# A speech joint's forward and backward pass on one core: row-layout fe by a transposing transfer, stores of out on GpSimd's queue, own tile for the g gradient, x ahead of grad_out, last w1 gradients together

## The chip, the cores and the metric

The kernel runs on one core of a Trainium2 chip. Times are device microseconds (us) of one execution. The core has TensorE (PE in the profile, with its weight loads as PEld), VectorE (DVE), ScalarE (ACT), GpSimd (POOL) and SyncE (SP), and sixteen DMA engines. A DMA is issued by SP, ACT or POOL; the transposing DMAs of this kernel are all issued by SP.

## The reference

Two strided convolutions over time with gelu, a joint of the result f with a second sequence g, and all gradients for a given grad_out:

```python
h = sum_i einsum(xp[:, i:i+T], w1[i]);  h = gelu(h)[:, ::2]
f = sum_i einsum(hp[:, i:i+T1], w2[i]); f = gelu(f)[:, ::2]
fe = f @ w_f          # (B, 4000, 256)
ge = g @ w_g          # (B, 8, 256)
j = tanh(fe[:, :, None] + ge[:, None])
out = j @ w_o         # (B, 4000, 8, 256)
# returned: out and the gradients of x, w1, w2, g, w_f, w_g, w_o
```

B = 2, T = 16000, D = 256, three taps, U = 8 rows of g, all bf16.

## The kernel before

**Tiling.** The 2 x 4000 rows of f are taken as one line of 8000 and cut into 17 chunks: one of 256, fifteen of 512, one of 64. Chunk 8 holds the border of the two batches. A chunk's rows stand in blocks of 128 (4 blocks in a full chunk). The channel axis has two halves of 128.

**Stages of a chunk.** `stage_a` (lines 500 to 564) does both convolutions, gelu and its derivative factors (G1o, G1e, G2), then fe with channels on partitions (tile FE), and from chunk 2 on (`NTR = 2`) calls `fe_rows`, which turns FE into rows (tile FER) by 8 TensorE transposes at line 575 and one eviction. HT, the activations, is turned into rows HR by a transposing DMA (`tile_rows`, line 485). `stage_j` (line 614) runs four times over pairs of u: tanh of FE with ge as bias (JT, line 630); the same tanh in row layout (JR): for chunks 0 and 1 by TensorE transposes of JT, later by adding FER and the broadcast ge rows GEB (line 653) and a tanh (line 658); the products for w_o's gradient (GWO), for the gradient of j (from GOT, grad_out transposed by a DMA), and for out, which is evicted into OUT_SB and stored (line 730) by SP. Buffers JR are 3, OUT_SB 3, GOT 3, grad_out (GO) 4. `stage_de` (line 796) does the backward convolutions: GN, its rows GNR by a transposing DMA, GH and its rows GHR, the weight gradients of w_f and w2 (`wgrad`), the gradient of x (GX_SB, stored by SP), and calls `grad_w1` (line 933) from x in rows (XR) and GHR. Each weight gradient is a PSUM sum of one chunk that VectorE adds into an fp32 accumulator (line 777); the last one is subtracted from the negated accumulator into a STAGE tile (line 768) and stored.

In the loop over k from line 1065 the body runs `stage_j` of chunk k, `stage_a` of chunk k + 1 and `stage_de` of chunk k - 1. After the last chunk, `grad_w1` of chunk 15 is run as the final one; that of chunk 16 comes before it as an ordinary accumulation.

**Order of the work.** Nothing is issued where it is written. Every operation is recorded with its engine, a cost, its data dependences and a due time, and `Flow.issue` (line 106) simulates the engines and the SP queue and emits the instructions in the order that the simulation gives. For SP it knows three kinds of transfers, T (transposing), L (load) and S (store), with bytes per ns, gaps between kinds (`TURN`) and a backlog limit per kind. That order is fixed at build time; at run time each engine takes its instructions in that order and waits for semaphores. A buffer of a class (`cls`, line 50) is used again once its last user is done.

**Other names.** GpSimd copies the halos, the block edges that a convolution reads from a neighbour (`halo`, line 414; the copies are at line 347). `make_ge_rows` (587) and `gg_out` (954) make the rows of ge and the gradient of g; both take a buffer of class `jr` for their small result. `load_xc` (360) loads x transposed (XC), chunk 1 in two parts; `load_go` and `load_got` load grad_out and transpose it; `load_xr` loads x as rows. At the start W1 and W2 come as six loads on ACT's queue. `evac` (317) moves PSUM to SBUF on ACT or DVE; all matmuls are recorded at line 312 (`mm`).

Of the kernel before, what the change touches and what calls it, by code (L numbers as in the profile page):

```python
# [20 lines left out]
class Buf:  # L21


    def __init__(self, cls, shape, dtype, name):
        self.cls, self.shape, self.dtype, self.name = cls, shape, dtype, name
        self.t, self.slot, self.log, self.users, self.seq, self.born = None, None, [], 0, None, None
# [5 lines left out]
class Op:  # L32
    __slots__ = ("eng", "cost", "fn", "deps", "succ", "left", "prio", "new", "bufs", "done", "xfer", "n", "ready")


class Flow:
# [4 lines left out]
    TURN = {"TL": 800.0, "TS": 800.0, "SL": 550.0, "LL": 350.0}  # L41
# [20 lines left out]
    def op(self, eng, cost, fn, r=(), w=(), new=(), at=None, xfer=None, after=()):  # L62
# [23 lines left out]
        deps.update(b.born for b in bufs if b.born is not None)  # L86
# [13 lines left out]
    def ring(self, prev, kind, work):  # L100

        if kind == "T":
            return (1.3 * work + 250.0, 0.0) if prev == "T" else (work, 0.0)
        return work, self.TURN.get((prev or "") + kind, 130.0)

    def issue(self):
# [6 lines left out]
        def put(o):  # L113
            o.ready = max((d.done for d in o.deps), default=0.0)
            for e in o.eng:
                avail[e].append(o)
# [4 lines left out]
        while left:  # L121
# [54 lines left out]
            for b in o.bufs:  # L176
                b.users -= 1
                if b.users == 0 and b.cls is not None:
                    slots[b.cls][b.slot][1] = o.done
# [29 lines left out]
def kernel(  # L209
# [28 lines left out]
    KT = 2  # L238
# [30 lines left out]
    for name, n in (("xc", 1), ("ht", 1), ("g1e", 2), ("g1o", 2), ("g2", 2), ("fe", 2),  # L269
                    ("fer", 2), ("gsq", 2), ("gs", 2), ("jt", 3), ("got", 3), ("go", 4), ("out", 3), ("jr", 3),  # L270
# [36 lines left out]
    NGR = fixed([U, B, D], BF16, "NGR")  # L307
    gT = [fixed([P, KT, U], BF16, f"gT{b}") for b in range(B)]
# [23 lines left out]
    def dma(q, out, in_, r, w, bytes_, new=(), transpose=False, load=False, at=None, after=(), land=1500.0):  # L332
# [6 lines left out]
        if transpose:  # L339
            c, work = 1020.0 + bytes_ / 1100.0, bytes_ / 306.0  # L340
        else:
            c, work = 600.0, bytes_ / 384.0
        c = {"SP": c, "POOL": 650.0, "ACT": 450.0}[q]
        return op(q, c, go, r=r, w=w, new=new, at=at, after=after, xfer=("T" if transpose else "L" if load else "S", work, land))
# [15 lines left out]
    def load_xc(g_, at, after=()):  # L360
# [4 lines left out]
        for n_, (b0, b1) in enumerate(cuts):  # L365
            dma("SP", lambda b0=b0, b1=b1: XC[:, b0:b1, :, :c.np].rearrange("p j k n -> p (j k) n"),
                lambda b0=b0, b1=b1: dram(xf, 4 * c.q0 - 1 + b0, 4 * c.nb, b1 - b0, c.np),
                r=[], w=[(XC, ("m", n_))], bytes_=(b1 - b0) * c.np * D * 2, new=[XC] if n_ == 0 else [], transpose=True, at=at,
                after=after, land=2500.0 if c.first else 1500.0)
# [6 lines left out]
    def load_go(g_, up, at, after=()):  # L376
# [4 lines left out]
            bytes_=c.W * 1024, new=[GO], load=True, at=at, after=after)  # L381
        st[g_].setdefault("GO", {})[up] = GO

    def load_got(g_, up, at):
# [3 lines left out]
        dma("SP", lambda: GOT[:, 0:c.nb, :, :, :c.np].rearrange("p a j k n -> p (a j k) n"),  # L388
# [4 lines left out]
    def load_xr(g_, at, after=()):  # L393
# [5 lines left out]
        if c.first:  # L399
            pool_zero(lambda: XR[0:1, 0:3, :], [], [(XR, "a")], new=[XR], at=at, n=768)  # L400
            dma("SP", lambda: XR[0:1, 3:nr, :].rearrange("p f d -> p (f d)"), lambda: dram(xf, 0, 24, nr - 3, 1),
                r=[], w=[(XR, "b")], bytes_=3072, load=True, at=at, after=after)
            for lo, hi in ((1, 16), (16, 128)):
                dma("SP", lambda lo=lo, hi=hi: flat(lo, hi), lambda lo=lo, hi=hi: dram(xf, r0 + 8 * lo, 8, nr, hi - lo),
                    r=[], w=[(XR, lo)], bytes_=(hi - lo) * nr * 512, load=True, at=at, after=after)
        else:
            dma("SP", lambda: flat(0, c.np), lambda: dram(xf, r0, 4 * c.nb, nr, c.np),
                r=[], w=[(XR, "m")], bytes_=c.np * nr * 512, new=[XR], load=True, at=at, after=after)
# [20 lines left out]
    def conv_gelu(g_, jobs, rd, h_buf, pre, ho, gname, gcls, gshape, gsave, news):  # L429
# [4 lines left out]
        if c.first:  # L434
# [18 lines left out]
        for mt in range(KT):  # L453
# [11 lines left out]
        G = buf(gcls, gshape, BF16, gname)  # L465
# [13 lines left out]
            out=full(G, go_), in0=full(s, so), in1=full(sq), op=ALU.mult), r=both(sk) + both(qk), w=[(G, ("g", 0)), (G, ("g", 1))], new=[G], at=late)  # L479
# [20 lines left out]
    def stage_a(g_, t0, dt):  # L500
# [50 lines left out]
        FE = S["FE"] = buf("fe", [P, KT, CW], BF16, "FE")  # L551
        for mt in range(KT):
# [6 lines left out]
            evac(lambda mt=mt: FE[:, mt, :c.W], lambda ps=ps: ps[:, :c.W], c.W, r=[ps], w=[(FE, mt)])  # L559
# [6 lines left out]
    def fe_rows(g_):  # L566
        c, S = chunks[g_], st[g_]
        nb, n_, FE = c.nb, c.np, S["FE"]
        FER = S["FER"] = buf("fer", [P, NB, D], BF16, "FER")
        ps = psum(BF16)  # L570

        def trs(e, ps=ps):
            for a in range(nb):
                for kt in range(KT):
                    nc.tensor.transpose(out=ps[:n_, (a * KT + kt) * P:(a * KT + kt + 1) * P],  # L575
                                        in_=FE[:, kt, a * n_:(a + 1) * n_], identity=ident[:])
# [10 lines left out]
    def make_ge_rows():  # L587

        rows = buf("jr", [P, 2, 2, D], BF16, "JR")
        for b in range(B):  # L590
# [5 lines left out]
            op("PE", c_pe([D] * 2), mms, r=[gT[b], WG], w=[ps], new=[ps] + ([rows] if b == 0 else []))  # L596
            evac(lambda b=b: rows[:U, b, 0], lambda ps=ps: ps[:U, :D], D, r=[ps], w=[(rows, b)])
        dma("POOL", lambda: GED[:].rearrange("b (u d) -> u b d", d=D), lambda: rows[:U, :, 0, :], r=[rows], w=[GED],
            bytes_=8192, land=2500.0)

    def load_geb(c, at):
        t_ = lambda: GED[:]
        for up in range(UP):
            for lo, hi, b in parts_of(c):
# [3 lines left out]
                    r=[GED], w=[(GEB, up)], bytes_=(hi - lo) * 1024, load=True, at=at(up))  # L608
# [5 lines left out]
    def stage_j(g_, t0, dt):  # L614
# [4 lines left out]
        def cut(ap, lo, hi):  # L619
            return ap.rearrange("p (a n) -> p a n", a=nb)[:, :, lo:hi] if c.mid else ap  # L620

        def pair(up):
# [4 lines left out]
            for j in range(2):  # L627
                for mt in range(KT):
                    for k_, (lo, hi, b) in enumerate(parts_of(c)):
                        op("ACT", c_act((hi - lo) * nb, ptr=True), lambda e, j=j, mt=mt, lo=lo, hi=hi, b=b: nc.scalar.activation(  # L630
                            out=cut(JT[:, j, mt, :W], lo, hi), in_=cut(S["FE"][:, mt, :W], lo, hi), func=ACT.Tanh,
# [98 lines left out]
            dma("SP", lambda dst_=dst_: dst_, lambda OUT=OUT: OUT[:n_, 0:nb].rearrange("p a u v -> p a (u v)"), r=[OUT], w=[],  # L730
# [65 lines left out]
    def stage_de(g_, t0, dt):  # L796
# [84 lines left out]
        load_xr(g_, t0 - 300.0 if c.last else t0 + dt * 0.3)  # L881
# [51 lines left out]
    def grad_w1(g_):  # L933
        c, S = chunks[g_], st[g_]
        nb, nx = c.nb, c.nx
        XR, GHR = S["XR"], S["GHR"]
        rows = lambda R, a, d2, m: R[:m, a, d2 * P:(d2 + 1) * P]
# [186 lines left out]
```

## Time and profile before

| | |
|---|---|
| median of three runs | 791.5 us (787.8 to 792.93) |
| the profiled execution | 793.2 us |
| its span, first to last instruction | 791.3 us, granted TensorE clock 0.992 |
| DMA in the span | 184.34 MB, mean 233 GB/s |
| SP's queue (q1) | 182.16 MB, 99.2% of 16 engines' time |
| GpSimd's queue (q0) | 0.41 MB |

Costly groups of instructions, by shape, with busy time and mean:

| line, engine | what | count | busy us | mean ns |
|---|---|---|---|---|
| L630 ACT | tanh JT from FE, 128x512 | 224 | 156.5 | 746 |
| L312 PE | out from JT and WO, 256 columns | 992 | 149.3 | 273 |
| L698 DVE | NGZ from JSQ and PSUM, 128x512 | 196 | 132.5 | 677 |
| L713 DVE | ZS + NGZ, fp32 128x1024 | 90 | 109.4 | 1215 |
| L653 DVE | JR from FER and GEB | 112 | 76.0 | 683 |
| L575 PE | transposes of FE | 112 | 8.5 | 219 |
| L321 ACT | FER from PSUM, 128x1024 | 14 | 14.5 | 1037 |

A matmul's duration overlaps with the next one's, so the spacing of starts says more of TensorE's pace than the mean. A wait for several semaphores is put down to the one that came last. In views by window the numbers after each engine's busy time are counts.

### The profile page before, as it was taken

What the parts mean: (1) busy time and instruction counts of PE and PEld (TensorE: products, weight loads), DVE (VectorE), ACT (ScalarE), POOL (GpSimd) and SP (SyncE); (2) the same over time, 40 slices, a digit from 0 to 9 for tenths busy, and PEclk for the clock granted to TensorE, in tenths of its full rate; (3) what the DMA queues carried; (4) which work ended last, traced back from release to release, by engine and by line L of the source; (5) the groups of instructions that cost most, each with busy time, mean ns of one, the idle gap of its engine ahead of it and who ended that gap; (6) DMA issues with size and microseconds to landing.
All of it is one profiled execution on the core that took longest, in us unless ns stands there. A gap on an engine that the chain in (4) does not pass through costs nothing. (4 is left out here: it accounts for less than half of the span.)

```text
span 791.3 us, 15382 instructions
## 1 busy us (share of the span) xinstructions
PE 770.7 (97%) x5620; PEld 534.6 (68%) x5620; DVE 725.1 (92%) x1519; ACT 711.1 (90%) x1134; POOL 88.2 (11%) x225
## 2 busy tenths in 40 slices
PE   8989989999999999999999998999999999999996
PEld 5756657676676766767566674676767667677765
DVE  4889989999999999999998987999999999999875
ACT  5999989989999999999999897998999999999752
POOL 3101110110102011010100201002020010201000
PEclk9999999999999999999999999999999999999999
DMA  9999999999999999999999999999999999899563
GB/s 204 236 239 223 232 226 257 236 234 277 226 283 222 245 247 221 259 222 255 253 229 251 244 268 230 208 257 214 272 243 239 247 219 276 196 247 249 156 180 94
DMA packets 396084, 184.34 MB, mean 233 GB/s; under 512 B 320350, under 2 KB 389768, under 8 KB 394088
## 3 DMA queue, kind: packets, MB, share of 16 engines
q1 hardware_dynamic: 394136, 182.16, 99.2%
q10 hardware_dynamic: 1632, 0.79, 0.4%
q8 instruction: 44, 0.72, 0.4%
q0 software_dynamic: 240, 0.41, 0.2%
q14 instruction: 32, 0.26, 0.1%
HBM read 52.99 MB, written 50.35 MB: 131 GB/s over the span
## 5 line engine op out<-in xcount | busy, mean ns | idle before, releaser
L630 ACT ACTIVATE JT<-FE,GE 128x512 bf16<-128x512 bf16 (+4 forms) x288 | 183.0, 686 | 0.1
L312 PE MATMUL ps<-WO,JT 128*128 128x256 bf16 (+1 forms) x1008 | 151.8, 273 | 0.3 <-DVE JR L326 0.2
L698 DVE SCALAR_TENSOR_TENSOR NGZ<-JSQ,ps 128x512 f32<-128x512 bf16 (+3 forms) x252 | 151.2, 607 | 0.4 <-PE ps L312 0.2
L312 PE MATMUL ps<-GOT,WOT 128*128 128x512 bf16 (+2 forms) x544 | 150.6, 362 | 0.8 <-ACT FE L321 0.4
L312 PEld LDWEIGHTS <-JT 128*128 128x128 bf16 (+1 forms) x1008 | 98.5, 98 | 62.1 <-issue 0.8
L321 ACT CAST OUT_SB<-ps 128x512 bf16<-128x512 f32 x200 | 119.8, 600 | 17.6 <-PE ps L312 17.1
L689 ACT ACTIVATE JSQ<-JT 128x1024 bf16<-128x1024 bf16 (+2 forms) x127 | 128.8, 1014 | 6.4 <-DVE NGZ L698 6.0
L312 PE MATMUL GWO<-GO_R,JR 128*128 128x256 bf16 (+1 forms) x1008 | 132.2, 274 | 0.0
L658 ACT ACTIVATE JR<-JR 128x1024 bf16<-128x1024 bf16 (+1 forms) x116 | 123.3, 1065 | 7.6 <-DVE JR L653 7.1
L713 DVE TENSOR_TENSOR ZS<-ZS,NGZ 128x1024 f32<-128x1024 f32 (+2 forms) x102 | 115.2, 1130 | 0.6
L312 PEld LDWEIGHTS <-JR 128*128 128x128 bf16 (+1 forms) x1008 | 98.9, 98 | 15.7 <-issue 0.7
L312 PEld LDWEIGHTS <-W 128*128 128x128 bf16 x636 | 60.7, 99 | 55.6 <-DMA W<-in_w_dram 1.5
L312 PE MATMUL ps<-W1T,GH 128*128 128x256 bf16 (+2 forms) x506 | 94.3, 325 | 0.0
L312 PE MATMUL ps<-XC,W 128*128 128x512 bf16 (+2 forms) x432 | 90.7, 351 | 0.0
L312 PE MATMUL ps<-GHR,XR 128*128 128x256 bf16 (+1 forms) x756 | 85.6, 273 | 0.7 <-ACT GHR L321 0.7
L777 DVE TENSOR_TENSOR ACC<-ACC,ps 128x512 f32<-128x512 f32 x90 | 61.0, 681 | 23.4 <-PE ps L312 23.0
L653 DVE TENSOR_TENSOR JR<-FER,GEB 128x1024 bf16<-128x1024 bf16 (+1 forms) x116 | 77.7, 673 | 4.2 <-DMA out_dram<-JR 4.2
L312 PEld LDWEIGHTS <-XR 128*128 128x128 bf16 (+1 forms) x756 | 73.8, 98 | 9.5 <-issue 0.8
L459 DVE SCALAR_TENSOR_TENSOR g_s<-g_sq,ps 128x512 bf16<-128x512 bf16 (+1 forms) x96 | 62.4, 653 | 11.9 <-ACT HT L457 10.8
L312 PEld LDWEIGHTS <-WOT 128*128 128x128 bf16 x544 | 50.9, 98 | 29.6 <-issue 2.0
L312 PE MATMUL ps<-GNR,HR 128*128 128x256 bf16 (+1 forms) x504 | 64.7, 273 | 4.5 <-DMA GNR<-GN 4.1
L455 ACT ACTIVATE g_sq<-ps 128x512 bf16<-128x512 f32 (+2 forms) x102 | 57.6, 565 | 12.2 <-PE ps L312 12.2
(128 smaller groups left out, 976.9 us busy)
## 6 DMA issues: line engine op xcount, KB each, us to landing
GO_R<-in_grad_out_dram SPq DMA_DIRECT2D x60, 512.0 KB
out_dram<-OUT_SB SPq DMA_DIRECT2D x60, 512.0 KB
XR<-in_x_dram SPq DMA_DIRECT2D x15, 1088.0 KB
out_dram<-GX_SB SPq DMA_DIRECT2D x30, 512.0 KB
out_dram<-STAGE SPq DMA_DIRECT2D x9, 128.0 KB
GOT<-GO_R SPq DMA_TRANSPOSE x68
GO_R<-in_grad_out_dram SPq DMA_DIRECT2D x4, 256.0 KB
GEB<-GED SPq DMA_DIRECT2D x8, 128.0 KB
```

The costliest lines, as they stand in the source:

```text
L312: nc.tensor.matmul(ps_ap, lhsT=lhsT, rhs=rhs, start=start, stop=stop)
L321: nc.scalar.copy(out=dst(), in_=src())
L455: op("ACT", c_act(W, True), lambda e, mt=mt, ps=ps: nc.scalar.activation(out=sq[:, 0:nb, mt, :n_], in_=blk(ps, c), func=ACT.Square, scale= ...
L459: op("DVE", c_dve(W), lambda e, mt=mt, ps=ps: nc.vector.scalar_tensor_tensor(out=s[:, so:so + nb, mt, :n_], in0=sq[:, 0:nb, mt, :n_], scal ...
L630: op("ACT", c_act((hi - lo) * nb, ptr=True), lambda e, j=j, mt=mt, lo=lo, hi=hi, b=b: nc.scalar.activation(out=cut(JT[:, j, mt, :W], lo, h ...
L653: op("DVE", c_dve(na * 2 * D, 0.5), lambda e, h=h, na=na, JR=JR: nc.vector.tensor_tensor(out=JR[:n_, 0:na], in0=S["FER"][:n_, 2 * h:2 * h ...
L658: op("ACT", c_act(na * 2 * D), lambda e, na=na, JR=JR: nc.scalar.activation(out=JR[:n_, 0:na], in_=JR[:n_, 0:na], func=ACT.Tanh), r=[JR], ...
L689: nc.scalar.activation(out=JSQ[:, :, :W], in_=JT[:, j, :, :W], func=ACT.Square)
L698: nc.vector.scalar_tensor_tensor(out=cut(Z[:, d2, :W], lo, hi), in0=cut(JSQ[:, d2, :W], lo, hi), scalar=1.0, in1=cut(ps[:, :W], lo, hi), o ...
L713: nc.vector.tensor_tensor(out=o_, in0=i0, in1=i1, op=ALU.add)
L777: op("DVE", c_dve(512), lambda e: nc.vector.tensor_tensor(out=acc_ap().rearrange("p k d -> p (k d)"), in0=acc_ap().rearrange("p k d -> p ( ...
```

## The change

- **fe_rows.** For all chunks but the last, FER comes from FE by a transposing DMA on SP's queue (`tile_rows`, due as before), instead of TensorE transposes and an eviction. FE is laid out by blocks of 128, [P, NB, KT, P], for this.
- **Stores of out** are issued by GpSimd, those of the last chunk by SP as before.
- **GGR**, a tile of its own, holds the rows of ge and of the g gradient, in place of JR buffers.
- **Start.** x of chunk 1 and W2 (one load, on SP) are due before the first grad_out loads.
- **last_w1.** The w1 gradients of chunks 15 and 16 are summed in one PSUM bank per tap and then go straight into the final subtraction.
- **G2** is computed in its own tile, with one more `gsq` buffer, and takes no `gs` buffer.
- **Planner.** Transposing transfers are reckoned at 234 bytes per ns, not 306; the gaps between kinds are new; two kinds of ordering without a data wait (`soft`, `behind`) are added; a slot is free at the latest end of its users.

```diff
-    TURN = {"TL": 800.0, "TS": 800.0, "SL": 550.0, "LL": 350.0}
+    TURN = {"TT": 250.0, "TL": 750.0, "SL": 900.0, "LL": 200.0, "TS": 250.0, "LS": 250.0, "SS": 400.0}
...
-        deps.update(b.born for b in bufs if b.born is not None)
+        o.soft = ({b.born for b in bufs if b.born is not None} | set(behind)) - deps - {o}
+        deps |= o.soft
...
-        if kind == "T":
-            return (1.3 * work + 250.0, 0.0) if prev == "T" else (work, 0.0)
-        return work, self.TURN.get((prev or "") + kind, 130.0)
+        return work, self.TURN.get((prev or "") + kind, 0.0)
...
-            o.ready = max((d.done for d in o.deps), default=0.0)
+            o.ready = max((d.done for d in o.deps if d not in o.soft), default=0.0)
...
+                b.free = max(b.free, o.done)
                 if b.users == 0 and b.cls is not None:
-                    slots[b.cls][b.slot][1] = o.done
+                    slots[b.cls][b.slot][1] = b.free
...
-                    ("fer", 2), ("gsq", 2), ("gs", 2), ("jt", 3), ("got", 3), ("go", 4), ("out", 3), ("jr", 3),
+                    ("fer", 2), ("gsq", 3), ("gs", 2), ("jt", 3), ("got", 3), ("go", 4), ("out", 3), ("jr", 3),
...
+    GGR = fixed([U, B, D], BF16, "GGR")
...
-            c, work = 1020.0 + bytes_ / 1100.0, bytes_ / 306.0
+            c, work = 1020.0 + bytes_ / 1100.0, bytes_ / 234.0
...
+        G = buf(gcls, gshape, BF16, gname)
+        here = gname == "G2"
+        if here:
+            sq, s = buf("gsq", [P, NB, KT, P], BF16, "g_sq"), G
+            so, scr = 0, [sq, G]
...
-        FE = S["FE"] = buf("fe", [P, KT, CW], BF16, "FE")
+        FE = S["FE"] = buf("fe", [P, NB, KT, P], BF16, "FE")
...
-            evac(lambda mt=mt: FE[:, mt, :c.W], lambda ps=ps: ps[:, :c.W], c.W, r=[ps], w=[(FE, mt)])
+            evac(lambda mt=mt: FE[:, 0:nb, mt, :n_], lambda ps=ps: blk(ps, c), c.W, r=[ps], w=[(FE, mt)])
...
         nb, n_, FE = c.nb, c.np, S["FE"]
+        if not c.last:
+            return tile_rows(g_, "FER", "fer", FE, nb, shape=[P, NB, D], land=2500.0)
...
-        dma("POOL", lambda: GED[:].rearrange("b (u d) -> u b d", d=D), lambda: rows[:U, :, 0, :], r=[rows], w=[GED],
+        dma("POOL", lambda: GED[:].rearrange("b (u d) -> u b d", d=D), lambda: GGR[:], r=[GGR], w=[GED],
...
-                            out=cut(JT[:, j, mt, :W], lo, hi), in_=cut(S["FE"][:, mt, :W], lo, hi), func=ACT.Tanh,
+                            out=cut(JT[:, j, mt, :W], lo, hi), in_=S["FE"][:, 0:nb, mt, lo:hi], func=ACT.Tanh,
...
-            dma("SP", lambda dst_=dst_: dst_, lambda OUT=OUT: OUT[:n_, 0:nb].rearrange("p a u v -> p a (u v)"), r=[OUT], w=[],
+            dma("SP" if c.last else "POOL", lambda dst_=dst_: dst_, lambda OUT=OUT: OUT[:n_, 0:nb].rearrange("p a u v -> p a (u v)"), r=[OUT], w=[],
...
+    def last_w1(i):
+        ps = psum()
+        two = [w1_terms(g_, i) for g_ in (LAST - 1, LAST)]
+        n = [0, KT * sum(len(t_) for t_ in two)]
+
+        def mms(e, terms):
+            for d2 in range(KT):
+                for lhs, rhs, _ in terms:
+                    mm(ps[:, d2 * D:(d2 + 1) * D], lhs(d2), rhs(), n[0] == 0, n[0] == n[1] - 1)
+                    n[0] += 1
...
+        acc_add(ACC1, i, lambda: ACC1[:, i], ps, LAST, out_2[i], True)
...
-            gg = buf("jr", [P, 2, 2, D], BF16, "JR")
-            evac(lambda gg=gg: gg[:U, 0, 0], lambda ps=ps: ps[:U, :D], D, r=[ps], w=[gg], new=[gg], scale=-1.0)
-            dma("SP", lambda b=b: out_4[b], lambda gg=gg: gg[:U, 0, 0], r=[gg], w=[], bytes_=4096)
+            evac(lambda b=b: GGR[:, b], lambda ps=ps: ps[:U, :D], D, r=[ps], w=[(GGR, b)], scale=-1.0)
+            dma("SP", lambda b=b: out_4[b], lambda b=b: GGR[:, b], r=[(GGR, b)], w=[], bytes_=4096)
...
-    for i in range(KK):
-        wload("ACT", W2, i, lambda i=i: W2[:, i], lambda i=i: w2[i].rearrange("(kt p) n -> p kt n", p=P), BIG + 1, 6500.0)
+    load_xc(1, BIG, 60.0)
+    dma("SP", lambda: W2[:].rearrange("p i k n -> p (i k) n"), lambda: w2.rearrange("i (kt p) n -> p (i kt) n", p=P),
+        r=[], w=[(W2, i) for i in range(KK)], bytes_=393216, load=True, at=BIG + 30.0, land=2500.0)
...
-                load_go(k, up, t0 + Wk * (up // 2 * 2 / UP - 0.6))
+                load_go(k, up, t0 + Wk * (up // 2 * 2 / UP - 0.6), [got_op[0, up - 2]] if k == 0 and up > 1 else ())
...
-            grad_w1(LAST - 1)
+            for i in range(KK):
+                last_w1(i)
```

## The prediction

> **What bounds the kernel now.** I read the page's first two parts, then busy time in windows, the order of TensorE's instructions in one chunk, the chain of waits, and the waits by engine. The page says that four resources are nearly full at once.
>
> ```profile
> PE 770.7 (97%) x5620; PEld 534.6 (68%) x5620; DVE 725.1 (92%) x1519; ACT 711.1 (90%) x1134; POOL 88.2 (11%) x225
> ...
> PEclk9999999999999999999999999999999999999999
> DMA  9999999999999999999999999999999999899563
> ```
>
> The windows separate them. Rows give us, then PE, PEld, DVE, ACT and POOL busy, clock, DMA share, GB/s. The second window is exactly one chunk.
>
> ```profile
> 10.00:20.00 10.00, 7.23 (x60) 4.95 (x58) 7.91 (x27) 6.63 (x18) 2.34 (x7) 0.83 1.05 200
> ...
> 551.00:598.35 47.35, 47.35 (x338) 32.54 (x337) 45.84 (x89) 44.91 (x68) 5.42 (x12) 1.00 1.04 254
> ...
> 40.00:50.00 10.00, 7.69 (x44) 4.37 (x43) 9.64 (x25) 9.30 (x15) 0.00 (x0) 0.87 1.03 267
> 780.00:791.30 11.30, 4.96 (x41) 3.81 (x40) 5.64 (x10) 1.77 (x3) 0.00 (x0) 0.86 0.37 100
> ```
>
> In the steady state TensorE has no gap in 47.35 us. VectorE has 1.5 us left, ScalarE 2.4. TensorE is at its pace there, not only marked busy: its instructions follow each other by what they stream.
>
> ```profile
> 555.39 0.61 PE L575 MATMUL psb<-ident,FE 128*128 128x128 bf16 x8
> 555.84 0.59 PE L312 MATMUL ps<-GOT,WOT 128*128 128x512 bf16 x2
> 556.27 0.60 PE L312 MATMUL ps<-WO,JT 128*128 128x256 bf16 x4
> ```
>
> Two matmuls of 512 columns and four of 256 both take 0.43 to 0.44 from start to start. The eight transposes of FE take 0.45. The chain of waits is TensorE alone from 487.7 to 784, and before that it holds one long DMA piece.
>
> ```profile
> 480.45 5.48 DMA out_dram<-JR
> 485.93 0.03 issue
> 485.96 0.02 DVEq L653
> 485.98 0.04 issue
> 486.02 0.69 DVE JR L653
> ...
> 487.71 1.01 PE ps L312 x2
> 488.72 1.71 PE GWO L312 x8
> ```
>
> Outside the steady state TensorE is idle 7.2 us in the first 50 us, 2.5 near 107, 1.3 near 393, 2.6 near 487, and about 6 at the end. The DMA queue is the doubtful one: its share is near 1 everywhere. But the share exceeds 1 (1.35 at 273 GB/s in 541 to 544, a stretch of transposes; 1.09 at 404 GB/s in 562 to 564, mostly copies), so 1 is not its ceiling. From 527 to 528 it falls to 0.20, and from 537 to 538 to 0.16, where SP stands at a semaphore with nothing issued. No PE wait from 500 to 740 is put down to a DMA. So TensorE bounds, and DMA is near.
>
> **Part 1, FE rows by a transfer.** Of chunks 2 to 15, 14 in all, each loses 8 transposes: 14 x 0.44 = 6.2 us of TensorE's time, on the path. ScalarE loses 14 copies of 1.037, 14.5 us, which were under TensorE. Each chunk gains one transposing DMA of 0.262 MB: 0.96 us at the 273 GB/s above, or 1.13 at the chunk's mean of 232. The cover for its latency: FE is ready at 555.0 (the second cast starts at 554.32 and takes 0.68), and no later add into JR that could need the new rows starts before 561.29, so at least 6.3 us. SP takes 1.2 to 2.9 us to issue such a transfer (least and median of GOT's), and moving it takes about 1. If HR's transfer (0.85 MB, about 3 us) stands in front, 6.3 us is just enough; each us over it stops VectorE, with 1.5 us a chunk to spare. I take nothing for it. The new block layout of FE leaves the tanh at 128x512; HT is already evicted in that layout at 604 ns against FE's 596, so nothing.
>
> **Part 2, stores of out on GpSimd's queue.** 64 stores leave SP, each about 0.60 of issue; 4 in a chunk give SP 2.4 us, about what the new transfer costs it. On GpSimd the trace shows DMA instructions of 0.59 to 0.76 us (WO, 128 KB: 0.72), so 4 in a chunk cost 3 us if size doesn't count and 4 x 2.9 = 11.5 if it scales to 512 KB. GpSimd is busy 5.4 of 47.35. Queued behind a store are the halo copies; the tightest reader I find is the first W2T matmul with halo, at 538.0, after GN's copies end at 534.3: 3.7 us of room. OUT has three buffers and a store is needed back about two pairs later, 2 x 11.8 = 23.7 us; a POOL load landed 6.9 us after issue. So I take nothing on the path, and keep the price on VectorE for a rival.
>
> One row bears on that. GpSimd's copy of two elements takes 0.19 when alone and 1.12 here, while VectorE runs an addition with two SBUF operands from 539.35 to 540.56:
>
> ```profile
> 539.49 1.12 POOL L347 COPY hGHe<-GH 128x2 bf16<-128x2 bf16 x1 [4.82 <-DVE GH L839]
> ```
>
> The Trainium skill, page "SBUF — State Buffer", section "Who interferes with whom", has it as an exclusive lock on a shared pair of ports: whichever of VectorE and GpSimd comes first blocks the other, and it advises against DMAs from GpSimd beside such work, since GpSimd writes their descriptors itself. By that rule this part would cost and not be free; the trace agrees for a copy, and has no store to show. How much is rival A, priced from rows below.
>
> **Part 3, an own tile for the g gradient.** VectorE's add into JR waited 4.2 us for the small store of the gradient to leave a JR buffer. It cost TensorE more than its 2.6 idle: the W2T pair and the 8 GWO matmuls, 0.43 + 0.87 at pace, ran from 484.95 to 490.43, so 5.48 - 1.30 = 4.2 lost, since the clock fell (0.89 in 480 to 490). Removed, next in line are SP's transfers of GNR and XC, behind which nothing waited there. I take 4.2; low end 2.6.
>
> **Part 4, x ahead of grad_out, and w2 in one load.** XC of chunk 1 lands in two parts, issued at 4.21 and 13.60, and its 48 convolution matmuls start at 24.30; they would now fill the holes from 10 to 25, and chunk 1's FE would come sooner, which ends the hole at 45 (TensorE waits for JT, 1.9 us). The grad_out loads and GOT fall behind. Against it: W2 now comes behind 1.1 MB of transposed x on SP's queue, and conv2 of chunk 0 already waits 1.36 us for W2 at 13.13. At 273 GB/s that is 4 us of transfers, no later than now; but the first half of XC took SP 6.63 us to issue, which would make it up to 5 later. From 20 on ScalarE is full, so most of the 7.2 us can't be won. Between +4 won and 5 lost I take 2 won.
>
> **Part 5, last w1 gradients together.** At the end three additions into ACC (784.79 to 786.69) stand between the last matmul and the three final subtractions. Both chunks now accumulate in one PSUM bank, the additions go, and the last matmul (785.63) is near enough: 1.9 us, low end 1.2.
>
> **The planner** gets other transfer costs, so each order changes. The two GNR waits (2.5 and 1.3) may go, or as many may come: plus or minus 3.8, taken as 0.
>
> Sum: 6.2 + 4.2 + 2 + 1.9 = 14.3. The profiled execution took 793.2 (span 791.3 and 1.9 around it), which gives 778.9; it stood 1.7 above the median of 791.5, so from the median 777.
>
> **Rivals.** *A, GpSimd's stores hold up VectorE.* Speaking for it: the row above; a VectorE op of 0.42 at 0.62 beside a GpSimd copy (37.58); VectorE has only 1.5 us a chunk. It decides from 1.5 / 4 = 0.38 us per store. At the 0.72 of WO's row, fully exposed, VectorE needs 45.8 + 2.9 = 48.7, which is 1.35 over the present chunk, x 15 = 20, less 8.1 from parts 3 to 5: 803. Against: GpSimd's 12 copies a chunk cost VectorE little now. *B, DMA becomes the bound.* If it is full at 232 GB/s, 1.13 us more a chunk x 14 = 16, less 8.1: 799. Against: the dips to 0.2, and 273 to 404 GB/s elsewhere. The Trainium skill, "DMA: Bandwidth & Descriptors", section "Issuing engines are not separate DMA queues", says that a second issuing engine buys no bandwidth, only issue time; nothing here measured two queues full. *C, the waits move.* FE rows late, W2 late, or more GNR waits take back 6 to 8 of the 14: 784. *D, the transposes go but another engine paces.* If VectorE's 45.8 and its waits hold the chunk at 47.1, half of the 6.2 stays away: 780; this lies inside the forecast.
>
> **How the numbers follow.** Forecast 0.57, C 0.18, B 0.11, A 0.14. Low end: 6.2 + 4.2 + 4 + 1.9 + 3.8 = 20.1, so 771, and 769 for the spread of runs. High end: B and a W2 that comes late lie near 800; A beyond it is left out. About 1% is what a measurement of this kernel can tell from no change: 783.6 and 799.4. Faster: the forecast and a third of C, 0.63. Same: the rest of C and half of B, 0.18. Slower: A and half of B, 0.19.
>
> **What would show it.** Right: no L575 transposes but the last chunk's 2; a chunk of 46.9 us with TensorE still full; no 5 us DMA piece at 480; no ACC additions after the last matmul; GpSimd's share up by 3 to 12 us a chunk. Wrong: TensorE gaps that end with VectorE or GpSimd (A), with a DMA (B, C), or a chunk still at 47.3 or above.

## The result, and the profile after

| | median us | lowest to highest | ratio to before, 95% interval |
|---|---|---|---|
| before, same chip | 792.2 | 787.8 to 796.5 | |
| changed | 805.4 | 798.7 to 808.9 | 1.0137 [1.0091, 1.0184] |

The forecast was 777 in 769 to 800. The change made the kernel slower by some 13 us (11 by the ratio). Medians and ranges here hold every execution, while ratios leave out those over 1.5% above the fastest of their kernel. The profiled execution, the slowest of the four, took 808.9 us with a span of 807.1. Line numbers are a little higher in the changed kernel: L313 is the matmul, L322 the eviction on ScalarE, L337 the transposing DMA, L339 the plain DMA, L662 the addition into JR.

The page, busy time and slices:

```profile
PE 767.7 (95%) x5508; PEld 527.1 (65%) x5508; DVE 719.4 (89%) x1508; ACT 701.3 (87%) x1128; POOL 127.7 (16%) x289
...
PEclk9999999999999999999999899999999999998999
DMA  8999999999999999999999999999999999999473
```

TensorE lost exactly 14 x 8 = 112 instructions, and 3.0 us of busy time. But its idle time in the span went from 791.3 - 770.7 = 20.6 to 807.1 - 767.7 = 39.4. So the span's 15.8 more are 18.8 of idle TensorE less those 3.0. The queues (packets, MB, share):

```profile
q1 hardware_dynamic: 376936, 153.72, 90.1%
q0 software_dynamic: 9200, 32.92, 12.7%
```

The mean over the span is 233 GB/s, as before. The quiet chunk, by windows (us, then PE, PEld, DVE, ACT and POOL busy with counts, clock, DMA share, GB/s):

```profile
155.22:202.12 46.90, 46.90 (x329) 32.10 (x328) 45.11 (x88) 44.18 (x68) 7.37 (x16) 1.00 1.06 251
```

That is the 46.9 that was forecast, with TensorE full, VectorE with 1.8 us left and 251 GB/s. Where nothing goes wrong the transfer of FE's rows does what it should. The waits by engine (us in total, times, longest) show what does go wrong:

```profile
PEld L313 <- DMA GNR<-GN: 18.0, 6, 7.4
DVE JR L662 <- DMA FER<-FE: 16.6, 5, 5.9
PE ps L313 <- DMA GNR<-GN: 12.7, 3, 7.0
```

Before, the waits for GNR were these, and the wait for FER is new (weight load and matmul see the same stalls, which are not to be added):

```profile
PEld L312 <- DMA GNR<-GN: 6.9, 5, 3.0
PE ps L312 <- DMA GNR<-GN: 4.1, 3, 2.5
```

The chain of waits, which before reached back to 473 and held one DMA piece, now reaches back to 95 and holds five:

```profile
272.96 7.77 DMA FER<-FE
...
371.73 6.55 DMA FER<-FE
...
443.56 10.37 DMA GNR<-GN
...
524.93 7.44 DMA FER<-FE
...
736.77 5.96 DMA GNR<-GN
```

The longest stall can be followed on SP's queue (start, us, then what it issues):

```profile
423.52 4.06 SPq L337 DMA_TRANSPOSE GOT<-GO_R  x1
427.68 1.32 SPq L339 DMA_DIRECT2D out_dram<-GX_SB  x1
429.09 0.56 SPq L339 DMA_DIRECT2D GO_R<-in_grad_out_dram  x1
429.75 0.95 SPq L339 DMA_DIRECT2D GEB<-GED  x1
430.76 0.56 SPq L339 DMA_DIRECT2D XR<-in_x_dram  x1
439.92 2.89 SPq L337 DMA_TRANSPOSE GOT<-GO_R  x1
...
443.56 5.08 SPq L337 DMA_TRANSPOSE GNR<-GN  x1
```

on GpSimd:

```profile
423.92 0.71 POOL L339 DMA_DIRECT2D out_dram<-OUT_SB  x1 [9.88 <-ACT OUT_SB L322]
432.27 0.71 POOL L339 DMA_DIRECT2D out_dram<-OUT_SB  x1 [7.64 <-PE GWO L313]
444.83 0.71 POOL L339 DMA_DIRECT2D out_dram<-OUT_SB  x1 [3.73 <-ACT OUT_SB L322]
```

and on TensorE:

```profile
453.97 1.89 PE L313 MATMUL ps<-GNR,HR 128*128 128x256 bf16 x8 [6.97 <-DMA GNR<-GN]
```

What moved in between stands in the trace's packet records (start, length, queue and size of each DMA packet): a transposing transfer moves in packets of 256 bytes, a grad_out load in 1024, a store from GpSimd's queue in 4096. GpSimd's store of 423.92 moves from 426.1 to 435.5, and beside it SP's GOT transfer of 423.52 takes from 425.3 to 435.0, 9.7 us; a GOT transfer of the kernel before with no store beside it (issued at 714.17) took 2.6. The grad_out load of 429.09 stands behind it in SP's queue. It moves from 435.4 to 439.8, in part beside the store of 432.27. SP has nothing more to issue from 431.3 and stands before the next GOT until the load has landed, 8.6 us. GNR comes behind that GOT in SP's order, so it leaves at 443.56, with the store of 444.83 beside it, and takes 10.4 us. In a quiet chunk GNR has 7.0 us from issue to its first matmul; here TensorE stops for 7.0.

The end of the kernel is as forecast: the last matmul ends at 803.0, nothing is added into ACC behind it, and 4.1 us remain, against 5.7 before.

### The profile page after: what moved, and what is told of

Its sections match the earlier page's. It is cut to its first block, busy times and chain, and to the rows that moved or that the text cites. A ratio compares the mean times of both kernels' runs of the same rounds, so it can differ in the third digit from the quotient of the medians.

```text
span 807.1 us, 15196 instructions
## 1 busy us (share of the span) xinstructions
PE 767.7 (95%) x5508; PEld 527.1 (65%) x5508; DVE 719.4 (89%) x1508; ACT 701.3 (87%) x1128; POOL 127.7 (16%) x289
## 3 DMA queue, kind: packets, MB, share of 16 engines
q0 software_dynamic: 9200, 32.92, 12.7%
## 4 chain that ended last, share of the span: by engine, by line
PE 58%; DVE 12%; ACT 10%; DMA 5%; issue 3%; DVEq 0%; SPq 0%; ACTq 0%
PE ps L313 50%; PE GWO L313 8%; DMA FER<-FE 3%; ACT JT L639 2%; DVE g_s L467 2%; ACT JSQ L698 2%; DMA GNR<-GN 2%; DVE NGZ L707 2%; ACT JR L667 2%; DVE ZS L722 1%; ACT HT L465 1%; ACT g_sq L463 1%; DVE JR L662 1%; DVE ACC L786 1%; ACT OUT_SB L322 1%
## 5 line engine op out<-in xcount | busy, mean ns | idle before, releaser
L639 ACT ACTIVATE JT<-FE,GE 128x512 bf16<-128x512 bf16 (+4 forms) x288 | 178.6, 668 | 0.0
L313 PE MATMUL ps<-WO,JT 128*128 128x256 bf16 (+1 forms) x1008 | 151.1, 273 | 2.6 <-DVE ACC L786 2.3
L313 PE MATMUL ps<-GOT,WOT 128*128 128x512 bf16 (+2 forms) x544 | 150.4, 362 | 3.2 <-DMA GOT<-GO_R 3.2
L667 ACT ACTIVATE JR<-JR 128x1024 bf16<-128x1024 bf16 (+1 forms) x116 | 121.5, 1048 | 25.8 <-DVE JR L662 25.7
L313 PEld LDWEIGHTS <-JT 128*128 128x128 bf16 (+1 forms) x1008 | 98.5, 98 | 65.7 <-issue 4.8
L698 ACT ACTIVATE JSQ<-JT 128x1024 bf16<-128x1024 bf16 (+2 forms) x125 | 126.4, 1011 | 10.8 <-DVE NGZ L707 8.0
L322 ACT CAST OUT_SB<-ps 128x512 bf16<-128x512 f32 (+1 forms) x199 | 116.7, 593 | 20.0 <-PE ps L313 19.5
L313 PE MATMUL GWO<-GO_R,JR 128*128 128x256 bf16 (+1 forms) x1008 | 131.0, 273 | 0.5 <-DVE JR L327 0.4
L339 POOL DMA_DIRECT2D out_dram<-OUT_SB x64 | 45.5, 710 | 505.6 <-ACT OUT_SB L322 153.7
L313 PEld LDWEIGHTS <-JR 128*128 128x128 bf16 (+1 forms) x1008 | 98.0, 98 | 16.2 <-DVE JR L327 0.7
L313 PEld LDWEIGHTS <-W 128*128 128x128 bf16 x636 | 60.9, 99 | 59.7 <-issue 2.9
L313 PE MATMUL ps<-W1T,GH 128*128 128x256 bf16 (+2 forms) x506 | 94.3, 325 | 0.0
L662 DVE TENSOR_TENSOR JR<-FER,GEB 128x1024 bf16<-128x1024 bf16 (+1 forms) x116 | 78.2, 674 | 16.7 <-DMA FER<-FE 16.6
L313 PE MATMUL ps<-XC,W 128*128 128x512 bf16 (+2 forms) x432 | 86.4, 351 | 0.7 <-ACT OUT_SB L322 0.7
L313 PE MATMUL ps<-GHR,XR 128*128 128x256 bf16 (+1 forms) x756 | 85.6, 273 | 0.9 <-ACT GHR L322 0.7
L313 PE MATMUL ps<-GNR,HR 128*128 128x256 bf16 (+1 forms) x504 | 65.8, 282 | 15.2 <-DMA GNR<-GN 12.7
L313 PEld LDWEIGHTS <-XR 128*128 128x128 bf16 (+1 forms) x756 | 73.7, 98 | 9.9 <-issue 1.3
L313 PEld LDWEIGHTS <-WOT 128*128 128x128 bf16 x544 | 51.1, 98 | 36.2 <-DMA GOT<-GO_R 3.7
L313 PEld LDWEIGHTS <-HR 128*128 128x128 bf16 (+1 forms) x504 | 50.2, 101 | 27.0 <-DMA GNR<-GN 18.0
```

What stands on the lines that cost most here:

```text
L313: nc.tensor.matmul(ps_ap, lhsT=lhsT, rhs=rhs, start=start, stop=stop)
L322: nc.scalar.copy(out=dst(), in_=src())
L339: eng_.dma_start(out=out(), in_=in_())
L662: op("DVE", c_dve(na * 2 * D, 0.5), lambda e, h=h, na=na, JR=JR: nc.vector.tensor_tensor(out=JR[:n_, 0:na], in0=S["FER"][:n_, 2 * h:2 * h ...
L667: op("ACT", c_act(na * 2 * D), lambda e, na=na, JR=JR: nc.scalar.activation(out=JR[:n_, 0:na], in_=JR[:n_, 0:na], func=ACT.Tanh), r=[JR], ...
L698: nc.scalar.activation(out=JSQ[:, :, :W], in_=JT[:, j, :, :W], func=ACT.Square)
```

## The experiments

Each was timed beside the kernel before on one chip (its median there was 792.5 to 794.3) and differs from the named kernel only by the edit shown or named (of longer edits the decisive lines are shown). "Order kept" means that the planner reckons as in the named kernel, so that every engine has the same order, and only the issuing engine of one kind of transfer differs. An "interval" below is the time between the first GOT matmuls of successive chunks, worked out from TensorE's records. Differences in us are between medians unless the ratios are named; the two can lie some 5 us apart. Each profile is one execution.

### Undoing parts of the changed kernel

**a_fer_pe**: FE rows by TensorE again.

```diff
-        if not c.last:
-            return tile_rows(g_, "FER", "fer", FE, nb, shape=[P, NB, D], land=2500.0)
```

> The changed kernel with FE turned into rows by TensorE again (8 transposes and one eviction a chunk), all else as changed. Theory 1 (the rows of FE arrive on SP's queue 6 to 8 us after issue, at the edge of VectorE's first addition): VectorE's 16.6 us of waits for FER are gone, TensorE gets its 6.2 us back; 792 to 799. Theory 2 (the second store queue delays SP's transfers, the late GNR of 7 and 4 us are its work): the GNR waits stay, FER was a symptom; 802 to 811. Theory 3 (the planner's new order does it): no better than 800.

810.55 us (800.7 to 820.9; 808.8 without the slowest of the four), 1.0163 [1.0072, 1.0253]. Even in the fastest execution, which is the profiled one, TensorE's waits for GNR are all still there (12.4 us in 3), and the last interval is 46.4, as in the changed kernel (47.0); 39.8 before. Taking this part out alone wins nothing.

**a_store_sp_sameplan**: stores of out on SP, order kept.

```diff
-                bytes_=W * 1024)
+                bytes_=W * 1024, real="SP")
```

> The changed kernel with the same order on every engine, but the stores of out issued by SP at the place in the order where GpSimd's stood. Theory 2: GNR's 10.4 us from issue to landing near 444 and its 6.0 near 737 fall to the 4 to 6 of before; 788 to 796. Theory 1: FER waits of 15 us or more stay, 800 to 810. Rival: SP, now with 60 more issues of 0.6 us, is later still; 806 to 815.

798.75 us (794.3 to 803.9), 1.0081 [1.0045, 1.0117]. The last interval is 39.8, the waits for GNR fall from 12.7 to 7.3 us and those for FER from 16.6 to 4.6; but the profile here is the fastest of ten executions and that of the changed kernel the slowest of four. By the medians the queue of the stores is worth about 7 of the 13, though SP's order was planned without them. By the ratios it is 4, and their intervals overlap, so this run alone doesn't show it; b_store_sameplan below does.

**a_store_sp**: the same, planned with the stores on SP.

```diff
-            dma("SP" if c.last else "POOL", lambda dst_=dst_: dst_,
+            dma("SP", lambda dst_=dst_: dst_,
```

> The changed kernel with the stores of out on SP, planned anew; FER still by transfer. If the stores alone are to blame: 791.1 of the kernel with both undone, less the 6.2 of the transposes: 783 to 788. If FER's transfer costs by itself: 793 to 800, near the 798.8 that the changed order gave with its stores on SP.

800.21 us (797.3 to 801.4), 1.0112 [1.0085, 1.0139]. VectorE waits 13.7 us for FER in 8 places.

**a_both**: a_store_sp and a_fer_pe together.

> The changed kernel with FE rows by TensorE and the stores of out on SP, planned anew: what is left is the g gradient's own tile, x ahead of grad_out, w1 together and the planner's new constants. Theories 1 and 2 together: 781 to 788, the 8 us of the other parts below the kernel before. Theory 3 (the new planner constants make a worse order): 793 or above, with GNR waits left.

791.05 us (788.7 to 793.6), 0.9949 [0.9923, 0.9974]. Against a_store_sp, the FE rows by transfer cost 9.2 us (13 by the ratios); against a_fer_pe, the stores on GpSimd's queue 17 by the ratios. The interval of a_both lies below both of theirs. With both undone the kernel is a little faster than before, but still far from what the other parts were to bring.

### One part alone on the kernel before

**b_ggr_w1**: own tile GGR and the last w1 gradients together.

> The kernel before with the g gradient's own tile and the last w1 gradients together, nothing else. By the prediction's terms 4.2 + 1.9 less: 786. Rival: the 4.2 us wait is replaced by the next late transfer (GNR), 789 to 792.

787.22 us (785.7 to 794.8), 0.9934 [0.9896, 0.9972]: 6.2 us won, from 2.2 to 8.3 by the interval; 4.2 + 1.9 = 6.1 were forecast. In its profile VectorE's wait for the small store is gone, and 3.9 us are left after the last matmul, 1.8 less than before.

**b_store_sameplan**: stores of out on GpSimd's queue, order kept.

```diff
-                bytes_=W * 1024)
+                bytes_=W * 1024, real=None if c.last else "POOL")
```

> The kernel before with the same order on every engine; only the stores of out are issued by GpSimd, at the place in the order where SP's stood. Theory S (a store on a second queue leaves as soon as its tile is ready and stands beside whatever SP's queue moves, so that now and then a load or a transposing transfer takes 7 to 11 us instead of 4 to 6): more loads of grad_out over 7 us than the 2 of 27 before, new waits for GNR, 797 to 808. Rival: only the changed order has places tight enough to suffer; 789 to 795.

806.83 us (803.7 to 811.8), 1.0207 [1.0157, 1.0256]: 14 us from the issuing queue alone. The largest single piece is the last interval, 46.8 against 39.8. SP's queue there:

```profile
722.41 1.06 SPq L339 DMA_DIRECT2D GO_R<-in_grad_out_dram  x1
723.65 0.52 SPq L339 DMA_DIRECT2D XR<-in_x_dram  x1
728.87 4.25 SPq L337 DMA_TRANSPOSE GOT<-GO_R  x1
733.22 2.11 SPq L337 DMA_TRANSPOSE GNR<-GN  x1
```

And before:

```profile
716.99 0.62 SPq L338 DMA_DIRECT2D GO_R<-in_grad_out_dram  x1
722.11 2.94 SPq L336 DMA_TRANSPOSE GOT<-GO_R  x1
725.14 2.09 SPq L336 DMA_TRANSPOSE GNR<-GN  x1
```

Before, from the load to the issue of GNR it took 725.14 - 716.99 = 8.2 us; here 10.8, and the load itself is issued 1.9 later after the chunk's first GOT matmul. By the packet records the GOT transfer ahead of the load takes 4.0 us here (720.2 to 724.2) and 2.6 before, and the GOT and GNR of the rows above, behind another store, move from 730.9 to 737.1, where before it was 723.3 to 729.0. GNR so comes late, and TensorE waits 4.0 us for it at 737.57. No matmul waits for GpSimd.

**b_fer**: FE rows by transfer (with FE's layout by blocks), planned with the old constants.

```diff
+        if not c.last:
+            return tile_rows(g_, "FER", "fer", FE, nb, shape=[P, NB, D], land=2500.0)
```

> The kernel before with the rows of FE by a transposing transfer on SP's queue, stores still on SP, planned anew with the old constants. Theory F (the transfer itself is too late: it stands behind HR and GOT and lands 6 to 8 us after issue): chunks of 46.9 us where nothing waits, but VectorE waits for FER and GNR later than before; 792 to 800. Rival (only the stores on GpSimd made it late): 6 us less than before, 784 to 789.

796.5 us (794.0 to 798.7), 1.007 [1.0045, 1.0096]. Quiet chunks take 46.9, so the 6.2 us are saved, but 4 us net are lost. VectorE's wait:

```profile
DVE JR L655 <- DMA FER<-FE: 13.0, 8, 3.9
```

**b_newplan**: the planner's new constants alone (`TURN`, `ring`, 234).

> The kernel before with the changed planner's transfer rate (234 bytes per ns) and gaps between kinds, nothing else. Theory 3 (the new constants make a worse order): 797 or above, with more waits for GNR or GOT. Rival: the order is as good as the old one, 788 to 795.

789.89 us (787.4 to 791.6), 0.9974 [0.9956, 0.9991]. The new constants don't cost; they may win 2.6 us.

**b_best**: the new constants, GGR and the last w1 gradients together.

> The kernel before with the planner's new constants, the own tile for the g gradient and the last w1 gradients together; stores on SP's queue, FE rows by TensorE, the start as before. If the gains of the parts add: 793 - 6.2 - 2.6 = 784, with 781 to 787. If the two share the same idle time: 787 to 790.

787.72 us (786.1 to 787.9), 0.9929 [0.9886, 0.9973]. By the medians, 5.1 us won, the 2.6 and the 6.2 don't add; the interval reaches 9.0 and doesn't exclude it.

### What about the second queue costs

**b_store_act**: as b_store_sameplan, but issued by ScalarE.

```diff
+                bytes_=W * 1024, real=None if c.last else "ACT")
```

> The kernel before in its own order, the stores of out of all chunks but the last issued by ScalarE instead of SP. Theory (any second queue lets the stores run beside the grad_out loads that SP waits for, so single loads land late and TensorE waits): 802 to 810, and the last interval 45 to 47 us as with GpSimd's queue. Rival (it is GpSimd's own queue, with its 3.6 KB packets, that delays the loads): 791 to 797, last interval 39 to 40 us. [...]

801.16 us (794.9 to 802.6), 1.0102 [1.0066, 1.0137], with a last interval of 45.0. So a second queue costs 8 us also without GpSimd; GpSimd's costs some 6 more (8 by the ratios), and the intervals of the two ratios don't overlap. ScalarE takes 0.54 us to issue a store, and its quiet chunks stay at 47.3 us, so these issues don't pace the kernel. The queues of this kernel (packets, MB):

```profile
q1 hardware_dynamic: 361368, 149.65, 87.1%
q10 hardware_dynamic: 34400, 33.30, 13.5%
```

Less what ScalarE's queue had before (1632 packets, 0.79 MB), the stores are 32768 packets of 0.99 KB, just as on SP's queue. On GpSimd's they are 9200 - 240 = 8960 packets of 3.63 KB. These are means with some packets of a few bytes; the data go in packets of 1024 and 4096 bytes.

**b_store_not_end**: as b_store_sameplan, on GpSimd's queue only before chunk 13.

```diff
+                bytes_=W * 1024, real="POOL" if c.i < 13 else None)
```

> The kernel before in its own order; stores of out on GpSimd's queue in the chunks before the 14th alone, SP's queue from there. Theory (the price of the second queue is paid in single places, the largest of them the last chunks, 7 us): 797 to 801. Rival (every chunk pays its part): 804 to 806, in proportion to the chunks.

803.87 us (792.4 to 813.7), 1.0077 [1.0031, 1.0123]. The last interval is 39.8 again, so that stall does belong to the stores of the last chunks. The ratio gives some 6 us of the price that is left, 799 us, which lies in the theory's 797 to 801, and its interval lies below that of b_store_sameplan. But the median is not there: the profiled execution (803.3 us) has a new stall elsewhere, 56.5 us for chunk 2's interval (50.1 before, and 49.1 in b_store_sameplan, whose stores there are issued alike), and executions lie 21 us apart. So a good part of the price belongs to the last chunks, in stalls whose places aren't fixed from one execution to the next; how the rest is spread stays open.

**b_land** and **b_land_samestore**: the planner is told that a grad_out load lands 4.5 us after its transfer, not 1.5; in the first the stores stay on SP, in the second GpSimd issues them, order kept.

```diff
-            bytes_=c.W * 1024, new=[GO], load=True, at=at, after=after)
+            bytes_=c.W * 1024, new=[GO], load=True, at=at, after=after, land=4500.0)
```

> The kernel before, with the planner told that a grad_out load lands 4.5 us after its transfer (1.5 before), so that on SP the load of a unit is followed by another load or a store before its GOT. Control for the next: stores stay on SP. 788 to 796.

> The same order as the control, stores of out issued by GpSimd. Theory (the store's price is a grad_out load that lands late while SP stands before its GOT, and GNR behind that): with more between load and GOT the price falls from 14 to at most 6, 792 to 800. Rival (the second queue costs by the mean share that it takes from every transfer): still 12 to 15 above the control, 801 to 810.

b_land: 790.71 us (788.3 to 794.0), 0.9961 [0.9939, 0.9984]. b_land_samestore: 799.14 us (796.4 to 802.7), 1.0072 [1.0045, 1.01]. The price of the queue falls from 14 to 8.4, between the two expectations. In the profiles (spans 795.6 and 788.4) one interval holds it all, 56.0 against 48.9. SP and GpSimd there, with the stores on GpSimd:

```profile
84.78 7.34 SPq L337 DMA_TRANSPOSE GOT<-GO_R  x1
92.22 2.00 SPq L339 DMA_DIRECT2D GO_R<-in_grad_out_dram  x2
104.25 4.33 SPq L337 DMA_TRANSPOSE GOT<-GO_R  x1
108.67 2.49 SPq L337 DMA_TRANSPOSE GNR<-GN  x1
...
92.05 0.71 POOL L339 DMA_DIRECT2D out_dram<-OUT_SB  x1 [5.11 <-ACT OUT_SB L321]
```

and TensorE:

```profile
113.19 1.89 PE L312 MATMUL ps<-GNR,HR 128*128 128x256 bf16 x8 [6.31 <-DMA GNR<-GN]
```

The packet records show what the store of 92.05 runs beside. It is not the two loads: it and the store before it (issued at 86.23) move from 91.1 to 102.6, and beside them the GOT transfer of 84.78, which takes from 89.3 to 100.6. The loads stand behind that transfer in SP's queue and move from 99.4 to 105.1. In b_land, where SP issues the stores, the same GOT transfer takes from 91.8 to 96.5, and the two loads and two stores follow it until 103.7. So a transposing transfer that took 4.7 us takes 11.3 beside the stores, SP waits 10.0 us for the load instead of 3.8, and TensorE 6.3 us for GNR. From 92 to 104 the mean is 195 GB/s against 252. With the larger distance between load and GOT this profile has one such place left, and it is no shorter.

### The start

**a_both_nostart**: a_both with x of chunk 1 loaded where the loop does it, w2 as ScalarE's loads, and no first load held behind GOT.

```diff
-    load_xc(1, BIG, 60.0)
-    dma("SP", lambda: W2[:].rearrange("p i k n -> p (i k) n"), ...
+    for i in range(KK):
+        wload("ACT", W2, i, ...
...
-        if 0 < k < LAST:
+        if k + 1 < NG:
             load_xc(k + 1, t0 - Wk * 0.3)
```

> The changed kernel with its FE rows by TensorE and its stores on SP (791.05 measured), and the start undone as well: x of chunk 1 where the loop puts it, w2 as ScalarE's loads, nothing held behind the first GOT transfers. If the start part costs: 784 to 787. If it gains the 2 us that I forecast: 792 to 794. If it does nothing: 790 to 792.

782.32 us (780.0 to 784.6), 0.9854 [0.9814, 0.9894], the fastest kernel of the study. The part was taken as a gain of 2; it costs 8.7 here (7.5 by the ratios, whose intervals don't overlap). TensorE's waits for GNR all but vanish:

```profile
PE ps L313 <- DMA GNR<-GN: 1.1, 2, 0.6
```

**after_nostart**: the same undone in the changed kernel.

> The changed kernel with the start alone undone: x of chunk 1 where the loop puts it, w2 as ScalarE's two loads, nothing held behind the first GOT transfers. FE rows by transfer and the stores of out on GpSimd's queue stay. If the start costs by itself what it cost without those two (791.1 - 782.3 = 8.8): 795 to 799. If that 8.8 was an accident of the one order that the planner found there: 802 to 808, as the changed kernel.

804.26 us (800.1 to 809.5), 1.0132 [1.007, 1.0194]: with the FE rows by transfer and the stores on GpSimd's queue, undoing the start shows no gain. VectorE there waits 20.7 us for FER.

**a_both_w2**, **a_both_xloop**, **a_both_nobehind**: in a_both only w2, only x of chunk 1, only the holding of the first loads is put back.

> The changed kernel with FE rows by TensorE and stores on SP (791.05), and of the start only w2 put back as two loads on ScalarE's queue; x of chunk 1 stays ahead and the first grad_out loads stay behind the GOT transfers. If w2 as one load of 393 KB on SP is what costs: 782 to 785. If it is x ahead of grad_out or the loads held behind: 789 to 792.

> The changed kernel with FE rows by TensorE and stores on SP (791.05), of the start only x of chunk 1 put back where the loop loads it; w2 stays one load on SP, the first grad_out loads stay behind the GOT transfers. If x ahead of grad_out is what costs (the first GOT matmul 5 us later): 782 to 786. If it is the loads held behind: 789 to 792. If both are needed, or the planner's later order decides: 786 to 789.

> The same kernel (791.05) with x of chunk 1 ahead and w2 as one load on SP, but the first grad_out loads and the first x rows no longer held behind the GOT transfers. If the holding is what costs: 782 to 786. If it is x ahead: 789 to 792. If both are needed, or the planner's later order decides: 786 to 789.

| put back | median us | range | ratio to before |
|---|---|---|---|
| nothing (a_both) | 791.05 | 788.7 to 793.6 | 0.9949 [0.9923, 0.9974] |
| w2 | 791.66 | 787.0 to 794.3 | 0.9966 [0.9938, 0.9994] |
| the holding | 789.23 | 788.1 to 792.9 | 0.9941 [0.9915, 0.9967] |
| x of chunk 1 | 784.13 | 782.8 to 785.3 | 0.9876 [0.9819, 0.9933] |
| all three | 782.32 | 780.0 to 784.6 | 0.9854 [0.9814, 0.9894] |

It is x ahead of grad_out: with x put back, all four executions lie below the ten of a_both, though the intervals of the two ratios just touch. The first GOT matmul comes at 21.6 (a_both), 24.5 (w2 back) and 26.0 (holding back), but at 17.1 and 16.4 where x is loaded by the loop. In the kernel without the holding the 5 us are still there at the third chunk (94.1 against 89.0). In a_both they are made up by then (88.8), but stalls for GNR follow at 160 and 250. Why the planner's later order is worse there stays open.

## Why the prediction failed, point by point

- **What bounds it** was right: TensorE is full in quiet chunks, which went from 47.35 to 46.90. What was wrong was to reckon as if no transfer came later than before. DMA didn't become a bound on the mean (233 GB/s in both spans; rival B not seen), but single transfers became late.
- **Part 2** is the largest failed step: "I take nothing on the path". Its cover was reckoned on GpSimd (issue time, halo copies) and for OUT's buffers, and all of that held: 0.71 us per store, and no matmul waits for GpSimd. What I didn't ask is what the store collides with once it needn't wait in SP's queue. It runs beside whatever SP's queue moves, and where that is a transposing transfer, this falls to about half its rate (last section); a grad_out load that SP stands waiting for, and GNR behind it, are late. Alone on the kernel before, the other queue costs 14 us [1.0157, 1.0256], and taking it out of the changed kernel with the order kept wins about 7 by the medians. That the other queue costs is shown; that the halved transposing transfers make up the whole of it is read from three places, and no run isolates it.
- **Part 1** was right in its first term and wrong in its latency: "I take nothing for it". I gave it 6.3 us of cover and called a transfer of HR in front "just enough". FE is ready at 614.3 in a quiet chunk, SP issues FER at 618.3, behind HR and GOT, and the rows land at 625.4: 11.1 us, and even there VectorE waits 0.3. The prediction had HR alone in front and about 1 us of moving. In 8 places of b_fer it waits 13.0 in all, so 6.2 saved became 4 lost.
- **Part 3 and part 5** were right: 6.1 forecast, 6.2 measured together (2.2 to 8.3), with 1.8 of it at the end of the trace, where 1.9 were forecast. VectorE no longer waits for the gradient's small store.
- **Part 4** had the wrong sign: 2 won were taken, with 5 lost as the end of the range. With the other two parts undone it loses 8.7, nearly all by x ahead; in the changed kernel its loss is hidden (1.2, within the runs' spread).
- **The planner**, taken as 0 of plus or minus 3.8: 2.6 won alone.
- **Rivals.** C, the waits move, named what happened: FE rows late and more waits for GNR. But it took back 6 to 8 of the 14.3, and some 27 were taken back (14.3 and the 13 lost). A, VectorE held up by GpSimd's port, isn't what happened: VectorE's additions into JR keep their 0.68 us (683 ns before, 684 after), GpSimd's issue of a store its 0.71, quiet chunks are at 46.9 with GpSimd's stores in them, and stores issued by ScalarE cost 8 us too.

The sum of what the parts do alone on the kernel before, 14 + 4 - 6.2 - 2.6 = 9.2, isn't the measured 13 either. Part 4 is not in it, since it was not run alone there. It seems that parts which lean on the same in-order queue cover or sharpen each other: taking FE's part alone out of the changed kernel wins nothing, and 9.2 us once the stores are back on SP. No run shows how.

Why are stores on GpSimd's queue 6 us dearer than on ScalarE's? The rows show packets of 3.63 KB against 0.99 KB, beside a queue of SP whose mean is 149.65 MB / 361368 = 0.41 KB. The Trainium skill, "DMA: Bandwidth & Descriptors", section "Queues, rings and completion order", says that each DMA engine takes turns between its queues by whole packets. If the profile's packets are those, the queue with larger packets would take more of each turn, and SP's transfers get less. The packet records don't bear this out: beside a store, SP's transposing transfers move 98 GB/s with ScalarE's stores and 95 to 111 with GpSimd's, and the store itself 137 against 91 to 115. No run here varies the packet size alone, and why GpSimd's queue is dearer stays open.

## What to carry to other kernels

A transfer moved to a queue of its own starts earlier, and the price is paid by whatever it then runs beside: look for the transposing transfers that it will meet, for the load behind them that an in-order queue stands waiting for, and for the consumer of the transfer behind that. Cost a transfer that replaces engine work by the time from its input being ready to its last byte, queue included (11 us here, of which its bytes are about 1), against the first reader. And test parts alone as well as undone: here the version without the transfer, the second queue and the early x keeps the rest and runs at 0.9854 [0.9814, 0.9894].

## What the runs showed of the hardware

**The clock falls after short idle times, which adds some 2 us to the wait.** The windows of the changed kernel around the stall at 447 to 454 (the clock is the third number from the end):

```profile
450.00:452.00 2.00, 0.00 (x0) 0.00 (x0) 0.00 (x0) 0.42 (x1) 0.17 (x1) 0.81 1.10 358
452.00:454.00 2.00, 0.03 (x1) 0.04 (x2) 0.00 (x0) 0.00 (x0) 0.00 (x0) 0.50 0.99 117
454.00:456.00 2.00, 2.00 (x9) 1.31 (x10) 0.11 (x1) 0.00 (x0) 0.00 (x0) 0.50 1.28 290
456.00:458.00 2.00, 2.00 (x6) 0.76 (x5) 1.52 (x3) 0.00 (x0) 0.00 (x0) 0.50 1.14 224
458.00:460.00 2.00, 2.00 (x11) 0.91 (x10) 0.54 (x1) 1.66 (x4) 0.00 (x0) 0.99 1.13 210
```

After the idle 7 us the work from 454 to 458 runs at 0.50, 2 us more. In a_both a wait of 2.5 us was enough:

```profile
162.00:164.00 2.00, 1.73 (x13) 1.41 (x14) 0.65 (x2) 1.22 (x2) 0.19 (x1) 0.81 1.04 266
164.00:166.00 2.00, 2.00 (x11) 1.40 (x10) 1.77 (x3) 0.00 (x0) 0.00 (x0) 0.50 1.01 191
166.00:168.00 2.00, 2.00 (x15) 1.42 (x13) 1.05 (x2) 0.00 (x0) 0.00 (x0) 0.84 1.01 256
```

From 163 to 167 the clock takes 0.38 + 1.00 + 0.32 = 1.7 us more. The Trainium skill, "TensorE: Matmul & The Clock Gate", section "Part 1: The HAM clock gate (the "warmup" mystery)", has the clock halved after an idle window of about 3.4 us and restored after about as much work. The 0.50 agrees, and so does the length: 1.7 us lost is 3.4 us at half clock. That 2.5 us of idle suffice is less than it states.

**A transposing transfer moves at about half its rate beside a store of another queue.** I took the packet records in stretches of half a us and kept those in which SP's queue moves transposing packets (over 0.3 of the engines' time) and next to nothing else (under 0.03). In the seven traces with stores on a second queue, 559 to 598 stretches without a store move 206 to 209 GB/s, and 80 to 117 with a store beside them (0.1 or more) 95 to 111. The store then moves 91 to 137, so the two together (189 to 235) move about what the transposing transfer moves alone. The loads and stores that SP's queue moves without a transposing transfer fall less, from 286 to 301 GB/s to 175 to 240. It is a local effect: the means over the spans of the kernel before and the changed one are alike.

**A busy share says nothing of the rate.** The first row is b_land_samestore with the GOT transfer beside a store, the other two are b_land, with loads and stores in turn and with transposing transfers alone:

```profile
96.00:98.00 2.00, 2.00 (x17) 1.47 (x15) 1.70 (x4) 2.00 (x5) 0.51 (x2) 1.00 1.45 102
96.00:98.00 2.00, 2.00 (x12) 1.03 (x11) 1.94 (x5) 2.00 (x5) 0.00 (x0) 1.00 1.16 358
106.00:108.00 2.00, 2.00 (x13) 1.13 (x12) 2.00 (x5) 1.82 (x3) 1.01 (x1) 1.00 1.29 89
```

The third row also shows that a transposing transfer can be slow for 2 us with no other queue beside it.
